# An attention opening with a choice per score job: distances added on TensorE or a mask multiplied on VectorE, under a new written order

## The chip, the core and the metric

The kernel runs on one core of one Trainium2 chip. A core has TensorE for matrix products (PE in the profile, with PEld for its loads of weights), VectorE (DVE), ScalarE (ACT), GpSimd (POOL) and SyncE (SP). Every engine works through its own queue in order and waits on semaphores for the others. Data come from the chip's memory by DMA; GpSimd issues the loads that change the number type on their way, SyncE and ScalarE the plain ones. The metric is the device time of the program in microseconds (us). Three runs of the kernel before took 213.77 to 213.87 us, with a median of 213.77; the profiled execution has a span of 212.0 us.

## The reference

There are two steps. The first is attention over 4 batches of 8 heads, 768 positions, head size 64, in which a query sees the 96 keys up to its own position and the first 8 keys of the sequence. A penalty grows with the distance:

```
rel  = pos[:, None] - pos[None, :]
keep = (pos[None, :] < n_global) | ((rel >= 0) & (rel < n_local))
dist = where(is_global & ~is_local, n_local, abs(rel))
scores = q @ k.T / sqrt(64) - slope[head] * dist,  -1e9 where not keep
a = exp(scores - max) / sum
attn = a @ v
```

The second is a feed-forward step on the result, seen as 3072 tokens of 512 values: `h = max(x @ w_in, 0)`, then `(h * h) @ w_out`, with a hidden width of 2048. All inputs and the output are float32; the kernel computes in float16 with float32 sums.

## The kernel before, in words

**Tiling.** The sequence of one batch is six tiles of 128 positions. A query tile needs two key tiles only: its own and "the one before", a mix (kb and vb) whose first 32 rows are the start of the sequence with its global keys and whose other 96 rows come from the preceding tile. Work goes by halves of a batch, three tiles each, eight halves in all. In every half attention is followed by the first layer (hps, L560), relu (hr, L584), square (h, L595) and second layer (yps, L609). From the second batch on, the attention of one half is spread between the matrix products of the previous half.

**The opening** is the first batch, both halves, with nothing to hide behind at first. It is cut into small jobs by tile, named by letter, tile and part, and the constant `OPENING` is the order in which TensorE gets them:
- `T` (turn_tile, L669): the q and k tiles are transposed on TensorE, and copied to qk by ScalarE and VectorE. T0 does tiles 0 and 1, which come in by plain loads and are cast on VectorE or ScalarE.
- `S..o` and `S..b` (score_tile): the scores of a tile against its own keys and against the tile before. ScalarE takes exp (L734). Distance and mask go in by one of two ways. Where `added` is true, eight matmuls (L714) of slope_id (a diagonal with the head's slope) and dmask16 (the distances, with a big number where masked) put the penalty into the sum ahead of the eight matmuls of q and k (L721); exp then writes the weights ph at once. Where it is false, exp writes ex, and two products on VectorE (L742) multiply it by the table mask. The eight matmuls of q and k use 64 rows of the array each, two at a time; all others use 128.
- `V` (fix_v, L202): copies that make vb for a tile.
- `A` (attend_tile, L760): weights times values, two head pairs at a time, then reciprocal (L770) and product (L772) on VectorE give tm.
- `X` (tile_to_x, L787): tm is transposed into xt.
- `F`, `G`, `D`, `E` (layer1, L560): first layer for some tiles and one quarter (F, D) or eighth (G, E) of the hidden width; quarter c needs the load c of w_in.

**Loads.** The constant `LOADING` is the order in which GpSimd issues the loads of q, k and v tiles (128 KB each as they land) and of the four quarters of w_in (c0 to c3). Four loads of w_out follow. Eight semaphores serve these loads in turn, so the ninth load waits until the first has landed. Two plain loads each from ScalarE and SyncE bring the first two tiles of q and k.

**The planner.** `Plan` decides everything else. Each operation has a cost in us for each engine that may do it, operations it needs, and a rank. `run` takes again and again the operation with the earliest possible start, ties by rank, on the engine where it ends first, and so fixes engine and order of all operations. TensorE's jobs and the loads stay in their written order. A first load that is a q or k tile has rank -3, the index tables (iota, L233 and L235) have rank -2, other loads a rank of their place among TensorE's jobs. From the iota come ident (L239), which the transposes need, then the distances (L244 to L255), slope_id, dmask16 and the masks (L271). The planner also puts fillers ahead of a job of TensorE (`warm`, L213 and L216): products of zeros that keep the array busy while it would idle, as many as its idle time by the plan allows up to 24 us, reckoned for the very first job from a fixed 1.0 us and halved in the first us. The fillers need ident and stand in the queue, so they run however late the job is by then.

Of the kernel before, what the change touches and what calls it, by code (L numbers as in the profile page):

```python
# [16 lines left out]

OPENING = """T0 T2 S0o S1o S2b V1 S1b A00 T3 V2 A01 S2o A10 S3o A11 A21 T4 X11 X01 S3b A20 X00 T5 X21 S4o  # L20
X20 X10 F1 S4b A31 G11 V3 G10 G01 F0 A41 X31 A30 G00 S5b A40 F3 X30 G30 F2 X41 V4 X40 S5o
G21 E10 E00 E11 A50 G20 A51 X50 G31 X51 E01 D0 D1"""

LOADING = """v1 q2 k2 k3 q3 v0 v2 q5 q4 k4 k5 c1 v3 c0 v4 c3 c2 v5"""

# [14 lines left out]
class Plan:  # L44
# [6 lines left out]


    HOP = 0.08

    def __init__(self, warm_from, warm_until):
        self.warm_from, self.warm_until = warm_from, warm_until
        self.queues = {"PE": [], "LOAD": []}
        self.rest = []
        self.free = {e: 0.75 for e in ("ACT", "DVE", "POOL", "SP")}
        self.landed = 4.2  # L60
        self.rank = 0
        self.banks = [[] for _ in range(8)]

    def pe(self, cost, emit, needs=(), takes=0, lag=0.24):
        self.rank += 1
        op = Op({"PE": cost}, emit, needs, self.rank, lag)
        op.takes, op.users = takes, [[op] for _ in range(takes)]
        self.queues["PE"].append(op)
        return op
# [11 lines left out]
        self.rest.append(op)  # L81
        return op

    def load(self, dur, emit, needs=(), rank=None, lag=2.6):
        rank = self.rank + 0.5 if rank is None else rank
        op = Op({"POOL": 0.92}, emit, needs, rank, lag, land=dur)
        self.queues["LOAD"].append(op)
        return op

    def ready(self, op):  # L90
        t = 0.0
        for n in op.needs:
            if n.done is None:
                return None
            t = max(t, n.done + self.HOP)
        if getattr(op, "takes", 0):
            banks = self.idle_banks(op.takes)
            if banks is None:
                return None
            t = max(t, banks[-1][0] + self.HOP)  # L100
        return t + op.wait

    def idle_banks(self, n):
# [5 lines left out]
    def run(self):  # L109
        order = []  # L110
        while self.rest or any(self.queues.values()):
            best = None
            for op in [q[0] for q in self.queues.values() if q] + self.rest:
                r = self.ready(op)
                if r is None:
                    continue
                e = min(op.costs, key=lambda e: max(r, self.free.get(e, 0.0)) + op.costs[e])
                c = (max(r, self.free.get(e, 0.0)), op.rank, e, op)
                if best is None or c[:2] < best[:2]:
                    best = c  # L120
            start, _, e, op = best
            end = start + op.costs[e]
            idle = self.free.get(e, self.warm_from)
            taken = self.idle_banks(op.takes) if getattr(op, "takes", 0) else []
            self.free[e] = end
            op.done = end + op.lag
            if op.land is not None:
                self.landed = max(end + 1.45, self.landed) + op.land
                op.done = self.landed + op.lag
            for q in self.queues.values():  # L130
                if q and q[0] is op:
                    q.pop(0)
                    break
            else:
                self.rest.remove(op)
            self.spare = 0.0
            for (_, i), users in zip(taken, op.users if taken else ()):
                self.banks[i] = users
            self.now = [i for _, i in taken]
            if taken and start < self.warm_until:  # L140
                self.spare = start - 0.1 - max(idle, taken[-1][0])
                self.spare *= 0.5 if start < self.warm_from + 5.0 else 1.0
            op.emit(e)
            order.append((start, end, e, op))
        return order
# [3 lines left out]
def kernel(  # L149
# [152 lines left out]
    def list_loads(x):  # L302
        r0 = x.half * HALF
        prev = halves[x.hb - 2] if x.hb >= 2 else None
        before = (prev.turned if prev else []) + ([*halves[x.hb - 1].turned, prev.x_ops[NPAIR - 1]] if x.hb > 3 else [])
        vbefore = [halves[x.hb - x.half - 3].attended[-1]] if x.hb >= 4 else []

        def rows(src, name, t, rank=None):
            def emit(e):
                dst = (x.bt.v[:, x.half * HT + t, :, 0:D] if name == "v"  # L310
                       else staged(x, name)[:, t, :, :])
                dma = nc.gpsimd.dma_start(out=dst, in_=src[x.b, :, r0 + t * P:r0 + (t + 1) * P, :]  # L312
                                          .rearrange("h p d -> p h d"))
                if x.hb > 3 and name == "sq" and t == 0:
                    for turn in halves[x.hb - 1].turns + halves[x.hb - 2].turns[-1:]:
                        behind(dma, turn)
                if name == "sk":
                    x.last_load = dma
            return plan.load(0.86, emit, vbefore if name == "v" else before, rank,
                             1.6 if x.hb == 0 else 2.6)  # L320

        if x.half == 0:
            def start(e):
                new_batch(x.bt)
                nc.vector.memset(x.bt.v[:, :, :, D:D + 1], 1.0)
            x.bt.op = plan.add({"DVE": 0.1}, start, vbefore, rank=0)
        if x.hb > 1:
            x.q_in = [rows(q, "sq", t) for t in range(HT)]
            x.k_in = [rows(k, "sk", t) for t in range(HT)]
            x.v_in = [rows(v, "v", t) for t in range(HT)]  # L330
        else:
            x.k_in, x.q_in, x.v_in = [None] * HT, [None] * HT, [None] * HT
            for t in range(HT):
                r = x.half * HT + t
                if r > 1:
                    for src, name, key, ops in ((k, "sk", "k", x.k_in), (q, "sq", "q", x.q_in)):
                        load_jobs[f"{key}{r}"] = lambda src=src, name=name, ops=ops, t=t: (
                            ops.__setitem__(t, rows(src, name, t, -3 if not plan.queues["LOAD"]
                                                    else None)))
                load_jobs[f"v{r}"] = lambda t=t: (  # L340
                    x.v_in.__setitem__(t, rows(v, "v", t)), x.v_in[t].needs.append(x.bt.op))
            return
        for l in x.v_in:
            l.needs.append(x.bt.op)
        x.bt.v_in = [*getattr(x.bt, "v_in", []), *x.v_in]
# [37 lines left out]
    def fix_v(bt, t0, t1):  # L383
        def emit(e):
            copy(e, bt.vb[:, t0 - 1:t1 - 1], bt.v[:, t0:t1])
            copy(e, bt.vb[0:GR, t0 - 1:t1 - 1], bt.v[0:GR, 0:1].to_broadcast(
                [GR, t1 - t0, H, D + 1]))
        op = plan.add({"DVE": 0.85}, emit, [bt.v_in[0], *bt.v_in[t0:t1]],
                      wait=0.0 if bt is batches[0] else 4.0)
        for t in range(t0, t1):  # L390
            bt.vb_ops[t] = op
# [56 lines left out]

    def score(x, k):
        for unit in [UNITS[x.half][u] for u in TOGETHER[x.half][k]]:  # L450
            score_unit(x, unit, unit[0] == UNITS[x.half][TOGETHER[x.half][k][0]][0])

    def score_unit(x, unit, fresh):
        bt, sp = x.bt, []

        def emit(e):
            sp.extend(bank([P, 4, P], FP32, "sp", h) for h in range(2))
            warm(sp[0].rearrange("p i c -> p (i c)"))
            for i, (a, r, before) in enumerate(unit):
                for h in range(2):  # L460
                    rows = slice(h * D, (h + 1) * D)
                    lhsT = (bt.kb[rows, a, r - 2, :] if before and r > 1
                            else bt.qk[rows, 1, r - before, a, :])
                    nc.tensor.matmul(sp[h][:, i, :], lhsT=lhsT, rhs=bt.qk[rows, 0, r, a, :],  # L464
                                     start=True, stop=True)
        job = plan.pe(0.182 * fresh + 0.057 * 4, emit,
                      [o for a in {a for a, _, _ in unit} for o in x.qk_ops[a]], 2)
        weigh_unit(x, unit, job, sp)

    def weigh_unit(x, unit, job, sp):  # L470
# [227 lines left out]
                copy(e, bt.kb[:, :, u - 1, 0:GR], bt.qk[:, 1, 0, :, 0:GR])  # L698
            kb_ops[u] = plan.add({"DVE": 0.65, "POOL": 1.2}, fix, [tile_ops[u][1], tile_ops[0][1]])

    def score_tile(r, before):
        bt = batches[0]
        st = tiles.setdefault(r, {"weighs": []})
        added = r < HT
        c0 = 2 * P if before else 0 if r == 0 else P

        def emit(e):
# [15 lines left out]
        needs = list(tile_ops[r]) + (slope_ops if added else [])  # L723
        if before:
            needs += [kb_ops[r - 1]] if r > 1 else tile_ops[r - 1]
        job = plan.pe(0.182 + NPAIR * 0.07 + added * H * 0.056, emit, needs, 2)
        exps = []
        st["ph", before] = phat_p.tile([P, 2, NPAIR, P], FP16, name="ph0", tag="ph0")
        for h in range(2):
# [18 lines left out]
    def attend_tile(r, a0):  # L748
# [13 lines left out]
        needs = st["weighs"][a0 // 2::2] + [bt.v_in[r]]  # L762
        if r > 0:
            needs.append(bt.vb_ops[r - 1] if r > 1 else bt.v_in[0])
        job = plan.pe(4 * len(kinds) * 0.035, emit, needs, 1)

        def norm(e):
            av = st["av", a0]
# [9 lines left out]
    def tile_to_x(r, a0):  # L778
        x, t, st = halves[r // HT], r % HT, tiles[r]

        def emit(e):
# [4 lines left out]
            for i in range(2):  # L786
                nc.tensor.transpose(out=trx[:, i, :], in_=st["tm", a0][:, i, :, :],  # L787
                                    identity=ident)
        job = plan.pe(2 * 0.07, emit, [st["norm", a0]], 1)
        op = plan.after(job, {"ACT": 0.29, "DVE": 0.25}, lambda e: copy(  # L790
            e, x.xt[:, a0:a0 + 2, t * P:(t + 1) * P], st["trx", a0]))
        for a in (a0, a0 + 1):
# [55 lines left out]
    for r in range(NT):  # L848
        jobs[f"T{r}"] = lambda r=r: turn_tile(r, 2 if r == 0 else 1)
        jobs[f"V{r}"] = lambda r=r: fix_v(batches[0], r, r + 1)  # L850
        jobs[f"S{r}o"] = lambda r=r: score_tile(r, False)
        jobs[f"S{r}b"] = lambda r=r: score_tile(r, True)
        for i in range(2):
            jobs[f"A{r}{i}"] = lambda r=r, i=i: attend_tile(r, 2 * i)
            jobs[f"X{r}{i}"] = lambda r=r, i=i: tile_to_x(r, 2 * i)
# [64 lines left out]
```

The softmax here doesn't subtract the row's maximum and nothing guards it: scores larger than these inputs give would overflow.

## Time and profile before

| | |
|---|---|
| median of three runs | 213.77 us |
| span of the profiled execution | 212.0 us |
| TensorE busy | 206.4 us, 97% |
| VectorE, ScalarE, GpSimd busy | 116.3, 122.5, 66.5 us |
| first transposes of T0 start | 5.89 us |
| first second-layer matmuls start | 44.11 us |

The page gives the time for which each engine was busy, then the chain of work that ended last. For a question about an opening of 44 us in a span of 212 the timeline of one engine is the better view: each line is a group of equal instructions with its start, its length, the line of the code, the operation, what is written and read, and in brackets the idle time before it and what ended that. A matmul's length includes the way through the array, and one starts before the last has ended; so the time that a group takes is read from the start of one group to the start of the next. 56 ns from start to start is a product of 128 columns at full rate.

### The profile page before, as it was taken

The page shows a single profiled execution, that of the slowest core. Times are in us where ns is not written, and L with a number is a line of the kernel's source. Part 1 is how long each engine was busy: PE and PEld are TensorE (multiplying, and loading weights), DVE is VectorE, ACT ScalarE, POOL GpSimd, SP SyncE. Part 2 cuts the span into 40 slices and gives each one's busy share as a digit, 9 for nine tenths or more (in the row PEclk, how much of TensorE's full clock was granted, in tenths as well). Part 3 has the DMA queues.
Part 4 walks back from the last instruction along what each step waited for, and adds up shares of the span by engine and source line. Part 5 has one row for each costly group of instructions (what it writes and reads, how often), then busy time and mean ns, then how long its engine had stood idle before and what let it go on. Part 6 is the DMA issues. An engine that isn't in the chain of part 4 may idle for free.

```text
span 212.0 us, 4795 instructions
## 1 busy us (share of the span) xinstructions
PE 206.4 (97%) x1902; PEld 127.6 (60%) x1902; DVE 116.3 (55%) x332; ACT 122.5 (58%) x252; POOL 66.5 (31%) x82
## 2 busy tenths in 40 slices
PE   6999999999999999999999999999999999999994
PEld 7877898755554665456644665456644665455553
DVE  8679878434681678319860778218860777114300
ACT  6899897735741994148811994248811994247421
POOL 8997343594001930094008600095000000000000
PEclk9999999999999999999999999999999999999999
DMA  6999999999954999599988995399941100320012
GB/s 175 167 164 197 199 198 209 163 154 169 179 162 136 118 152 145 136 121 178 142 112 128 168 152 111 91 125 174 153 120 77 53 19 19 90 99 2 0 53 99
DMA packets 106343, 27.06 MB, mean 128 GB/s; under 512 B 96976, under 2 KB 103376, under 8 KB 106320
## 3 DMA queue, kind: packets, MB, share of 16 engines
q0 software_dynamic: 74944, 13.11, 80.0%
q1 hardware_dynamic: 30320, 13.11, 27.4%
q10 hardware_dynamic: 1056, 0.52, 0.8%
q8 instruction: 15, 0.25, 0.5%
q14 instruction: 8, 0.07, 0.1%
HBM read 27.26 MB, written 6.29 MB: 158 GB/s over the span
## 4 chain that ended last, share of the span: by engine, by line
PE 88%; POOL 6%; DMA 5%; DVE 0%; ACT 0%; issue 0%; POOLq 0%
PE hps L560 39%; PE yps L609 38%; DMA w_in_sb<-in_moe_w_in_dram 5%; PE sp L464 4%; PE av L519 4%; POOL v L312 2%; POOL sk L312 2%; POOL sq L312 2%; PE yps L637 2%; PE trp L411 1%; PE av L760 1%; POOL w_in_sb L369 0%; PE trx L787 0%; PE sp L721 0%; DVE ident L239 0%; ACT y L200 0%
## 5 line engine op out<-in xcount | busy, mean ns | idle before, releaser
L560 PE MATMUL hps<-xt,w_in_sb 128*128 128x384 f16 (+2 forms) x608 | 88.0, 301 | 0.1
L609 PE MATMUL yps<-w_out_sb,h 128*128 128x512 f16 x368 | 83.0, 379 | 0.0
L560 PEld LDWEIGHTS <-w_in_sb 128*128 128x128 f16 x608 | 53.9, 98 | 26.9 <-DMA w_in_sb<-in_moe_w_in_dram 0.4
L584 ACT ACTIVATE hr<-hps 128x384 f16<-128x384 f32 (+1 forms) x107 | 55.3, 525 | 13.8 <-PE hps L560 12.0
L609 PEld LDWEIGHTS <-h 128*128 128x128 f16 x368 | 34.9, 98 | 39.0
L200 ACT COPY y<-yps 128x512 f32<-128x512 f32 (+1 forms) x25 | 14.2, 568 | 66.5 <-PE yps L609 56.8
L595 DVE TENSOR_TENSOR h<-hr 128x768 f16<-128x768 f16 (+1 forms) x70 | 35.4, 521 | 24.5 <-ACT hr L584 24.0
L312 POOL DMA_DIRECT2D sq<-in_q_dram x22 | 19.5, 897 | 67.1 <-DMA xt<-tm 63.9
L477 ACT ACTIVATE ex<-sp 128x512 f16<-128x512 f32 x66 | 35.1, 624 | 1.2 <-PE sp L464 1.2
L586 DVE TENSOR_SCALAR hr<-hps 128x384 f16<-128x384 f32 x15 | 8.3, 554 | 38.7 <-PE hps L560 38.7
L312 POOL DMA_DIRECT2D v<-in_v_dram x24 | 21.5, 927 | 4.7 <-DMA w_out_sb<-in_moe_w_out_dram 3.7
L497 DVE TENSOR_TENSOR phat<-ex,mask 128x1024 f16<-128x1024 f16 (+1 forms) x36 | 20.3, 598 | 2.1 <-ACT ex L477 2.1
L312 POOL DMA_DIRECT2D sk<-in_k_dram x22 | 19.5, 910 | 3.4 <-DMA w_out_sb<-in_moe_w_out_dram 2.9
L529 DVE TENSOR_TENSOR tm<-av,rec 128x384 f16<-128x384 f32 x24 | 13.4, 558 | 0.8
L202 DVE COPY vb<-v 128x520 f16<-128x520 f16 (+1 forms) x32 | 10.2, 318 | 3.2 <-DMA v<-in_v_dram 2.7
L519 PEld LDWEIGHTS <-phat 128*128 128x128 f16 x240 | 9.8, 98 | 3.1
L519 PE MATMUL av<-v,phat 128*128 128x65 f16 x144 | 10.9, 194 | 0.0
L519 PE MATMUL av<-vb,phat 128*128 128x65 f16 x96 | 10.1, 194 | 0.0
L464 PEld LDWEIGHTS <-qk 64*128 64x128 f16 x168 | 6.3, 94 | 4.6 <-issue 3.7
L464 PE MATMUL sp<-qk 64*128 64x128 f16 x168 | 8.8, 218 | 0.0
L202 DVE COPY kb<-qk 128x96 f16<-128x96 f16 (+4 forms) x56 | 7.9, 205 | 0.8 <-ACT qk L200 0.4
L527 DVE RECIPROCAL rec<-av 128x6 f32<-128x6 f32 x24 | 4.7, 195 | 6.7 <-PE av L519 6.2
(66 smaller groups left out, 137.8 us busy)
## 6 DMA issues: line engine op xcount, KB each, us to landing
out_dram<-y SPq DMA_DIRECT2D x23, 256.0 KB, 2.2
v<-in_v_dram POOLq DMA_DIRECT2D x24, 128.0 KB, 7.0
sq<-in_q_dram POOLq DMA_DIRECT2D x22, 128.0 KB, 5.7
sk<-in_k_dram POOLq DMA_DIRECT2D x22, 128.0 KB, 6.3
w_in_sb<-in_moe_w_in_dram POOLq DMA_DIRECT2D x4, 512.0 KB, 10.5
w_out_sb<-in_moe_w_out_dram POOLq DMA_DIRECT2D x4, 512.0 KB, 15.7
y<-in_k_dram ACTq DMA_DIRECT2D x2, 256.0 KB, 4.5
y<-in_q_dram SPq DMA_DIRECT2D x2, 256.0 KB, 4.0
```

What stands on the lines that cost most here:

```text
L200: nc.scalar.copy(out=out, in_=in_)
L202: eng(e).tensor_copy(out=out, in_=in_)
L312: dma = nc.gpsimd.dma_start(out=dst, in_=src[x.b, :, r0 + t * P:r0 + (t + 1) * P, :] .rearrange("h p d -> p h d"))
L464: nc.tensor.matmul(sp[h][:, i, :], lhsT=lhsT, rhs=bt.qk[rows, 0, r, a, :], start=True, stop=True)
L477: nc.scalar.activation(out=st["ex"][:, h], in_=sp[h], func=AF.Exp, scale=scale)
L497: eng(e).tensor_tensor(out=x.phat[a][:, :, t0:t0 + n], op=ALU.mult, in0=st["ex"][:, :, i0:i0 + 2 * n].rearrange("p e (t b) c -> p e t (b c ...
L519: nc.tensor.matmul(av[:, h, j, :], lhsT=lhsT, rhs=rhs, start=not before, stop=before or r == 0)
L529: nc.vector.tensor_tensor(out=st["tm"].rearrange("p t e d -> p e t d"), in0=av[:, :, :, 0:D], in1=rec[:, :, :, None].to_broadcast([P, 2, H ...
L560: nc.tensor.matmul(st["ps"][:, i * n:(i + 1) * n], lhsT=w_in_sb[:, kk, m * P:(m + 1) * P], rhs=x.xt[:, kk, c0:c1], start=kk == 0, stop=kk ...
L584: nc.scalar.activation(out=o, in_=i, func=AF.Relu)
L595: eng(e).tensor_tensor(out=x.h2[:, m0:m0 + width, c0:c1], in0=hr, in1=hr, op=ALU.mult)
L609: nc.tensor.matmul(st["ps"], lhsT=x.h2[:, m, j * P:(j + 1) * P], rhs=w_out_sb[:, m, :], start=m == 0, stop=m == NFT - 1)
```

## The change

`score_tile` gets `added` from the name of the job: a plus sign in `OPENING` (S0o+) means that TensorE adds the distances, none that VectorE multiplies by the mask. Before, the tile's number decided it. The order in `OPENING` and `LOADING` is written anew. The copies for vb in the first batch may go to GpSimd where the planner finds that this ends earlier. And the planner's costs are set anew: score jobs, attend jobs and transposes, a saving where two half-row jobs meet, the lag of a load until it can be used, and a load that waits for the eighth load before it.

It is meant to use whichever of TensorE and VectorE has room at each score job, and to give the planner a truer picture to order by.

```diff
-OPENING = """T0 T2 S0o S1o S2b V1 S1b A00 T3 V2 A01 S2o A10 S3o A11 A21 T4 X11 X01 S3b A20 X00 T5 X21 S4o
-X20 X10 F1 S4b A31 G11 V3 G10 G01 F0 A41 X31 A30 G00 S5b A40 F3 X30 G30 F2 X41 V4 X40 S5o
-G21 E10 E00 E11 A50 G20 A51 X50 G31 X51 E01 D0 D1"""
+OPENING = """T0 T2 S0o+ S2b T3 S1b+ S1o+ V2 A01 S2o+ S3o+ A10 A11 V1 S3b+ A21 A20 A00 T4 X21 X11 X01 X10
+T5 X20 S4o X00 A30 A31 S4b S5b F0 G00 S5o X30 X31 G01 G10 G11 F2 V3 A40 F1 A41 G21 V4 G20 F3
+X40 A50 A51 X41 G30 E10 X50 E11 X51 E01 D1 G31 D0 E00"""
-LOADING = """v1 q2 k2 k3 q3 v0 v2 q5 q4 k4 k5 c1 v3 c0 v4 c3 c2 v5"""
+LOADING = """q2 k2 k3 q3 v0 q5 v2 v1 k5 q4 k4 v3 c0 c1 c2 v4 c3 v5"""
...
     HOP = 0.08
+    SWITCH = 0.12
...
-    def load(self, dur, emit, needs=(), rank=None, lag=2.6):
+    def load(self, dur, emit, needs=(), rank=None):
         rank = self.rank + 0.5 if rank is None else rank
+        lag = 2.25 if len(self.queues["LOAD"]) < 5 else 2.85
...
+        if op.land is not None and len(self.loads) >= 8:
+            t = max(t, self.loads[-8].done)
...
+            if e == "PE":
+                end -= self.SWITCH * (op.begins and self.half_rows)
+                self.half_rows = op.ends
...
-        op = plan.add({"DVE": 0.85}, emit, [bt.v_in[0], *bt.v_in[t0:t1]],
+        op = plan.add({"DVE": 0.85, "POOL": 1.7} if bt is batches[0] else {"DVE": 0.85}, emit, [bt.v_in[0], *bt.v_in[t0:t1]],
...
-        job = plan.pe(0.182 * fresh + 0.057 * 4, emit,
-                      [o for a in {a for a, _, _ in unit} for o in x.qk_ops[a]], 2)
+        job = plan.pe(0.36, emit, [o for a in {a for a, _, _ in unit} for o in x.qk_ops[a]], 2,
+                      begins=True, ends=True)
...
-    def score_tile(r, before):
+    def score_tile(r, before, added):
...
-        added = r < HT
...
-        job = plan.pe(0.182 + NPAIR * 0.07 + added * H * 0.056, emit, needs, 2)
+        job = plan.pe(0.38 + added * 0.53, emit, needs, 2, begins=not added, ends=True)
...
-        job = plan.pe(4 * len(kinds) * 0.035, emit, needs, 1)
+        job = plan.pe(4 * len(kinds) * 0.0305, emit, needs, 1)
...
-        job = plan.pe(2 * 0.07, emit, [st["norm", a0]], 1)
+        job = plan.pe(2 * 0.06, emit, [st["norm", a0]], 1)
...
-        jobs[f"S{r}o"] = lambda r=r: score_tile(r, False)
-        jobs[f"S{r}b"] = lambda r=r: score_tile(r, True)
+        for added in ("", "+"):
+            jobs[f"S{r}o{added}"] = lambda r=r, added=added: score_tile(r, False, bool(added))
+            jobs[f"S{r}b{added}"] = lambda r=r, added=added: score_tile(r, True, bool(added))
```

More of the change, by code (lines that the diff above doesn't have):

```diff
@@ L60, in __init__, with pe @@
         self.landed = 4.2
+        self.loads = []
+        self.half_rows = False
         self.rank = 0
         self.banks = [[] for _ in range(8)]
-    def pe(self, cost, emit, needs=(), takes=0, lag=0.24):
+    def pe(self, cost, emit, needs=(), takes=0, lag=0.24, begins=False, ends=False):
         self.rank += 1
         op = Op({"PE": cost}, emit, needs, self.rank, lag)
+        op.begins, op.ends = begins, ends
         op.takes, op.users = takes, [[op] for _ in range(takes)]
@@ L129, in run @@
                 op.done = self.landed + op.lag
+                self.loads.append(op)
             for q in self.queues.values():
@@ L318, in emit @@
                     x.last_load = dma
-            return plan.load(0.86, emit, vbefore if name == "v" else before, rank,
-                             1.6 if x.hb == 0 else 2.6)
+            return plan.load(0.86, emit, vbefore if name == "v" else before, rank)
         if x.half == 0:
@@ L450, in score, with score_unit @@
         for unit in [UNITS[x.half][u] for u in TOGETHER[x.half][k]]:
-            score_unit(x, unit, unit[0] == UNITS[x.half][TOGETHER[x.half][k][0]][0])
-    def score_unit(x, unit, fresh):
+            score_unit(x, unit)
+    def score_unit(x, unit):
         bt, sp = x.bt, []
```

## The prediction

> **What bounds the kernel now.** I began with the busy times of the page, went to the chain that ended last, and then took the opening apart on the timeline of TensorE.
>
> ```profile
> PE 206.4 (97%) x1902; PEld 127.6 (60%) x1902; DVE 116.3 (55%) x332; ACT 122.5 (58%) x252; POOL 66.5 (31%) x82
> PE 88%; POOL 6%; DMA 5%; DVE 0%; ACT 0%; issue 0%; POOLq 0%
> ```
>
> TensorE is busy 97% of the span and is 88% of the chain. The rest of the chain, POOL and DMA, lies in the first 23 us. After 36.25 us I find no pause between matmul starts longer than the change of row grouping, so whatever the opening gains or loses passes to the end whole. The timeline of TensorE shows where the opening loses time (start, us, then the group; a start is when the group began):
>
> ```profile
> 5.89 0.63 PE L669 MATMUL trp<-ident,sq 128*128 128x128 f16 x4
> ...
> 7.60 0.89 PE L216 MATMUL trp<-ident,zero 128*128 128x128 f16 x13
> 8.32 0.39 PE L669 MATMUL trp<-ident,sq 128*128 128x128 f16 x4
> 9.11 0.40 PE L669 MATMUL trp<-ident,sk 128*128 128x128 f16 x4 [0.40 <-DMA sk<-in_k_dram]
> 9.35 0.61 PE L714 MATMUL sp<-dmask,slope_id 128*128 128x128 f16 x8
> 9.89 0.40 PE L721 MATMUL sp<-qk 64*128 64x128 f16 x8
> 10.22 0.62 PE L714 MATMUL sp<-dmask,slope_id 128*128 128x128 f16 x8
> ...
> 44.11 5.34 PE L609 MATMUL yps<-w_out_sb,h 128*128 128x512 f16 x24
> ```
>
> T0's 16 transposes take 5.89 to 7.60, 107 ns each; the 13 fillers after them take 0.72 us, 56 ns each. T2's second half then waits: 8.32 + 4 x 0.056 = 8.55, but it starts at 9.11, 0.56 us later. The list of waits for the first 60 us names what holds the weight loads:
>
> ```profile
> PEld L669 <- DMA sk<-in_k_dram: 0.8, 2, 0.6
> PEld L787 <- DVE tm L772: 0.5, 2, 0.3
> PEld L560 <- DMA w_in_sb<-in_moe_w_in_dram: 0.4, 1, 0.4
> ```
>
> Taken as pauses between matmul starts, from T0's end (7.60) to the first second-layer matmul (44.11) these are: sk 0.57 and 0.24, tm 0.21 twice, w_in 0.27, and 0.15 + 0.04 in attend jobs: 1.69 us idle. Fillers are 0.84. So of 36.51 us, 33.98 are work, and **at most 2.5 us can be won** if the work stays.
>
> The timelines of GpSimd and of the chain show the supply:
>
> ```profile
> 0.84 0.34 POOL L233 IOTA dist<- 128x256 f32 x1 [0.39 <-POOLq L901]
> 1.14 0.13 POOL L235 IOTA pidx<- 128x1 f32 x1
> 1.67 1.04 POOL L312 DMA_DIRECT2D v<-in_v_dram  x1 [0.40 <-DVE ident L239]
> 2.70 0.91 POOL L312 DMA_DIRECT2D sq<-in_q_dram  x1
> ```
>
> ```profile
> 13.07 9.78 DMA w_in_sb<-in_moe_w_in_dram
> 22.90 1.94 PE hps L560 x24
> ```
>
> The iota comes ahead of the first load, and the second w_in quarter lands at about 22.9.
>
> **What the Trainium skill says.** (1) "TensorE: Matmul & The Clock Gate", Part 1: the array runs at half rate until a free-running window of about 3.4 us has been busy. The trace agrees in kind: 107 ns a transpose until 7.6, 56 after, 5.9 us after the first filler at 1.67. (2) "DMA: Bandwidth & Descriptors", Queues, rings and completion order: each DMA engine takes turns between queues, packet by packet. The trace shows no even turns: the software queue's first load is issued by 2.71, yet from 2 to 5 us only the hardware queues moved data, and from 6 to 8 the software queue alone moved a steady 154 GB/s. (3) "GPSIMD Engine Reference", 4.1 Engine selection: one-input elementwise work is roughly line-rate on GpSimd. No copy on GpSimd is in this trace.
>
> **The change, part by part.**
>
> *Added distances.* Before, five score jobs add them (40 rows of L714): S0o, S1o, S1b, S2o, S2b. After, six: S0o, S1b, S1o, S2o, S3o, S3b. TensorE gets 8 x 0.056 = +0.45. VectorE loses one net job of two products (L742), 2 x 0.38 = -0.75 between 17 and 33 us. Changing the row grouping costs about 0.10 on entry (9.35 + 0.45 = 9.80, seen 9.89) and 0.12 on exit; S2b now follows S0o's half-row matmuls and S5b follows S4b, which saves 2 x 0.22 = 0.44. Net work: 0.0, so 34.0 us remain.
>
> *Order of loads.* v1 gives up the front. A tile takes 131 KB / 154 GB/s = 0.85 us. k2, third before, becomes second: landing 9.11 - 0.85 = 8.25, if the software queue is still held up by the hardware loads. The first w_in quarter moves behind one more value tile: about 19.3 (it was needed then, at 19.31) to at most 20.1-20.4. The second lands at 22.9 as now, the third 2.55 later at 25.4.
>
> *A side effect.* The first load has a rank of -3 when it is a q or k tile, so it is issued ahead of the iota (rank -2). The iota then waits 0.9 us for that issue on GpSimd's in-order queue, and ident, the fillers and the mask arithmetic wait with it: first filler 1.67 + 0.9 = 2.6. The planner's own arithmetic still asks for about 41 fillers before T0, since it reckons from a fixed 1.0 us: 41 x 0.107 = 4.3, T0 at 6.9 instead of 5.89. If the clock again rises at 7.6, six or seven transposes run at 107 ns and nine or ten at 56: T0 ends at about 8.13, **0.5 later**. The casts, done by about 6.5, hide.
>
> *T2 to S2b.* The planner's landing for k2 leaves about 9 fillers, 0.5 us. T2 at 8.63 finds k2 landed and ends at 9.08; S0o starts there, 0.27 ahead of 9.35. But S2b now comes second instead of third and needs kb of tile 1. In the trace T0's VectorE evacuations end 1.1 after T0, those of ScalarE 1.5, and the kb copies another 0.8: 7.60 + 1.5 + 0.8 = 9.93. Shifted by 0.53 this is 10.45 with T2's evacuation fitted in, while S0o is done at 9.08 + 0.76 = 9.84: **a new wait of 0.6**. Behind it T3 and every later job stand in TensorE's queue.
>
> *Middle.* From S2b to F0 I add 9.7 us of work (score jobs 0.22 to 0.89, attend jobs 0.14 or 0.25, transposes 0.45 or 0.11): F0 at 10.45 + 9.7 = 20.15, plus about 0.2 for k4, which comes eleventh instead of tenth. That meets the first w_in quarter at 20.1-20.4. Another 5.05 of work brings F2 to 25.4, on the landing of the third. From F2 18.1 of work remain: 25.5 + 18.1 = 43.6.
>
> *V on GpSimd.* On VectorE a pair of copies takes 0.7 to 0.86 us. The page puts one-input work at line rate and two-input work at about twice VectorE's time, so I bound it by 0.7 from below and 1.7 from above, and take 1.5 as an estimate. Queued behind it are loads, but eight are in flight by then and POOL already idles 1.6 to 1.9 us between them for w_in landings: that wait hides it. Nothing is charged.
>
> *New costs in the planner* (score units at 0.36, eight loads in flight, lags) move only the placing of operations. Nothing in the later stages waits now, so zero, with +0.3 as the other end.
>
> Sum: 44.11 becomes about 43.65 with 0.1 of small waits: **-0.45 us, 213.3**.
>
> **Rivals.**
> 1. *Fillers and cold clock eat it.* Should the clock rise late, at 9 instead of 7.6, T0 and T2 lose another 0.5 and S2b starts near 11.0. For it: T0's lateness is no longer covered by the wait for sk. Against: four equal runs. Time 213.8.
> 2. *A new wait in the middle: slower.* ScalarE is busy 4.64 of 5 us from 10 to 20 and VectorE 4.61 of 5 from 15 to 20; seven score jobs in a run need 14 exponentials of 0.49 and hold two banks each. One job's lag (1.0) on top of the forecast gives 43.65 + 1.0 = 44.65: 214.3. Against: VectorE has 0.75 less to do.
> 3. *The software queue starts earlier with its first issue*, by up to 0.83 us, so that all landings shift; S2b's wait shrinks when evacuations go well and the w_in floor drops: 1.2 won, 212.6. Against: the hardware loads hold it up at 5.2 to 5.9.
>
> **How the numbers follow.** Forecast 0.42, rival 1 0.22, rival 2 0.20, rival 3 0.16. The forecast lies just beyond 0.2% (0.43 us): 0.3 of its 0.42 and rival 3 are faster, 0.46. Same: 0.12 of the forecast and most of rival 1, 0.30. Slower: rival 2 and the tail of rival 1, 0.24. The range reaches from rival 3 to rival 2: 212.6 to 214.3. It takes in the copy (nil), the later stages (+0.3) and the clock (+0.5).
>
> **What would show it.** First load ahead of the iota; first filler near 2.6; T0 near 6.9; a pause of about 0.6 ahead of S2b's L721; F0 near 20.3 and F2 near 25.4, both released by w_in; first L609 matmul near 43.65. It is wrong if T0 starts at 5.9 as now, if the software queue moves data by 3 to 4 us, or if pauses over 0.3 released by ScalarE or VectorE stand between 12 and 20.

## The result and the profile after

The changed kernel takes 214.44 us (median of five runs; a sixth, in which TensorE was slow from beginning to end, took 548 us and is left out) against 213.77 before: a ratio of 1.0032, 95% interval 1.0018 to 1.0046. It is slower by 0.7 us; 213.3 was forecast, and 214.44 lies just outside the range of 212.6 to 214.3. The profile shown here is of a second series of the same code, with a span of 212.6 us (212.0 before).

> The changed kernel as it is, for a profile in which TensorE runs at its usual rate. Theory 1 (the opening starts late: the first load goes ahead of the iota, and 41 fillers hold T0): first filler near 3.0 us, T0 at 7.3 to 7.5 instead of 5.9, T0's end at 8.2 to 9.1, first second-layer matmul near 44.7. Theory 2 (a stall in the middle, ScalarE or VectorE): T0 costs little, and pauses of over 0.5 us in sum released by ScalarE or VectorE stand between 12 and 22 us. Ratio 1.002 to 1.005.

This second series gave 214.59 us, ratio 1.0035 [1.0021, 1.0049]. Its page, first the busy times, then the chain by engine:

```profile
PE 205.7 (97%) x1909; PEld 127.6 (60%) x1909; DVE 116.3 (55%) x329; ACT 121.4 (57%) x251; POOL 67.9 (32%) x84
PE 94%; ACT 3%; POOL 1%; issue 1%; DVE 0%; POOLq 0%; ACTq 0%
```

The busy times have hardly moved, and they could not tell the two kernels apart. In the chain, DMA has vanished and ScalarE, which had 0%, has 3%: that is the first hint. The timeline of TensorE, in the same columns as before:

```profile
3.04 4.52 PE L227 MATMUL trp<-ident,zero 128*128 128x128 f16 x41 [3.04 <-DVE ident L250]
7.36 0.42 PE L679 MATMUL trp<-ident,sq 128*128 128x128 f16 x4
8.29 0.67 PE L227 MATMUL trp<-ident,zero 128*128 128x128 f16 x9
8.79 0.39 PE L679 MATMUL trp<-ident,sq 128*128 128x128 f16 x4
9.01 0.39 PE L679 MATMUL trp<-ident,sk 128*128 128x128 f16 x4
9.23 0.61 PE L723 MATMUL sp<-dmask,slope_id 128*128 128x128 f16 x8
...
10.43 0.40 PE L730 MATMUL sp<-qk,kb 64*128 64x128 f16 x8
...
21.67 1.93 PE L570 MATMUL hps<-xt,w_in_sb 128*128 128x128 f16 x24
...
44.78 1.46 PE L619 MATMUL yps<-w_out_sb,h 128*128 128x512 f16 x6
```

The second-layer matmuls begin at 44.78 instead of 44.11, and this 0.67 is as large as the difference of the medians. The wait for the k tile (0.56 before) is gone: T2's second half follows its first after 0.22. From T0's end to the second layer it is 44.78 - 8.29 = 36.49 us; before it was 36.51. So the pauses that went came back elsewhere, and T0's end moved from 7.60 to 8.29. By this sum alone the late T0 would be the whole loss; the first experiment asks whether it is. The list of waits of the weight loads says where to look (us in total, times, longest):

```profile
PEld L769 <- ACT ph L743: 0.6, 2, 0.4
PEld L730 <- ACT qk L211: 0.4, 1, 0.4
```

TensorE now waits for exponentials and for the evacuation of transposes, both by ScalarE. And GpSimd, which issues the loads, begins thus:

```profile
1.24 1.02 POOL L323 DMA_DIRECT2D sq<-in_q_dram  x1 [0.80 <-POOLq L911]
```

The first load is ahead of the iota (which follows at 2.35), as forecast, but it begins at 1.24, where the iota had begun at 0.84.

### The profile page after: what moved, and what is told of

Same layout as the page of the kernel before. It is cut to its first block, busy times and chain, and to the rows that moved or that the text cites. A ratio compares the mean times of both kernels' runs of the same rounds, so it can differ in the third digit from the quotient of the medians.

```text
span 546.4 us, 4811 instructions
## 1 busy us (share of the span) xinstructions
PE 540.2 (99%) x1909; PEld 241.1 (44%) x1909; DVE 119.6 (22%) x329; ACT 127.3 (23%) x251; POOL 67.8 (12%) x84
## 4 chain that ended last, share of the span: by engine, by line
PE 99%; POOL 0%; issue 0%; ACT 0%; DVE 0%; POOLq 0%
PE hps L570 42%; PE yps L619 40%; PE sp L474 4%; PE av L529 4%; PE yps L647 2%; PE trp L227 1%; PE trp L679 1%; PE sp L723 1%; PE av L769 1%; PE sp L730 1%; PE trp L421 1%; PE trx L796 1%; POOL sq L323 0%; PE sp L224 0%; POOL dist L244 0%
## 5 line engine op out<-in xcount | busy, mean ns | idle before, releaser
L570 PE MATMUL hps<-xt,w_in_sb 128*128 128x384 f16 (+2 forms) x608 | 232.3, 613 | 0.0
L619 PE MATMUL yps<-w_out_sb,h 128*128 128x512 f16 x368 | 223.5, 836 | 0.0
L570 PEld LDWEIGHTS <-w_in_sb 128*128 128x128 f16 x608 | 99.5, 172 | 116.8 <-issue 102.9
L619 PEld LDWEIGHTS <-h 128*128 128x128 f16 x368 | 62.4, 173 | 139.4 <-issue 135.8
L596 DVE TENSOR_SCALAR hr<-hps 128x384 f16<-128x384 f32 (+1 forms) x16 | 9.0, 566 | 136.7 <-PE hps L570 136.7
L529 PEld LDWEIGHTS <-phat 128*128 128x128 f16 x240 | 21.9, 147 | 10.3 <-issue 9.2
L529 PE MATMUL av<-v,phat 128*128 128x65 f16 x144 | 22.5, 289 | 0.0
L474 PE MATMUL sp<-qk 64*128 64x128 f16 x168 | 19.0, 366 | 0.0
L474 PE MATMUL sp<-qk,kb 64*128 64x128 f16 x96 | 15.4, 371 | 0.0
L227 PE MATMUL trp<-ident,zero 128*128 128x128 f16 x50 | 7.6, 373 | 3.0 <-DVE ident L250 3.0
```

What stands on the lines that cost most here:

```text
L227: nc.tensor.transpose(out=ps[:, 0:n], in_=zero[:, 0:P], identity=ident)
L529: nc.tensor.matmul(av[:, h, j, :], lhsT=lhsT, rhs=rhs, start=not before, stop=before or r == 0)
L570: nc.tensor.matmul(st["ps"][:, i * n:(i + 1) * n], lhsT=w_in_sb[:, kk, m * P:(m + 1) * P], rhs=x.xt[:, kk, c0:c1], start=kk == 0, stop=kk ...
L619: nc.tensor.matmul(st["ps"], lhsT=x.h2[:, m, j * P:(j + 1) * P], rhs=w_out_sb[:, m, :], start=m == 0, stop=m == NFT - 1)
```

## The experiments

All ratios are to the kernel before, measured beside each kernel. Differences in us from the changed kernel are taken from its second series, 214.59; against the first, 214.44, they are 0.15 smaller. "F0" is the first first-layer matmul, "layer 2" the first second-layer one, both from the trace.

### Is it the late start?

My theory was first that the load ahead of the iota delays the fillers, T0 and all that follows. The rival was a wait in the middle.

```diff
-                            ops.__setitem__(t, rows(src, name, t, -3 if not plan.queues["LOAD"]
+                            ops.__setitem__(t, rows(src, name, t, -1 if not plan.queues["LOAD"]
```

> Alone the rank of the first load is changed from -3 to -1, so that the iota goes ahead of it; 40 fillers before T0 instead of 41. Theory 1: T0 at 5.9 again, S2b about 1 us earlier, 0.6 to 1.2 us faster than the changed kernel and 0 to 0.5 us faster than the kernel before: 213.2 to 213.8. Theory 2: no more than 0.2 us from the changed kernel, 214.2 to 214.5.

Measured: 214.70, ratio 1.0041 [1.0028, 1.0054]. The iota came first, S2b started at 10.00, 0.4 us earlier, and yet F0 was at 21.96 and the time not better (TensorE of e1):

```profile
10.00 0.40 PE L730 MATMUL sp<-qk,kb 64*128 64x128 f16 x8 [0.29 <-DVE kb L213]
...
21.96 1.94 PE L570 MATMUL hps<-xt,w_in_sb 128*128 128x128 f16 x24
```

So undoing the late start alone won nothing, and my first theory fell. What held the work is on ScalarE's timeline (e1, 10 to 17 us):

```profile
15.79 1.57 ACT L743 ACTIVATE ph<-sp 128x512 f16<-128x512 f32 x3 [1.96 <-PE av L769]
```

and in the changed kernel itself, 10 to 22 us:

```profile
12.73 2.10 ACT L743 ACTIVATE ph<-sp 128x512 f16<-128x512 f32 x4
15.76 3.04 ACT L743 ACTIVATE ph<-sp 128x512 f16<-128x512 f32 x6 [0.93 <-PE av L769]
18.64 1.13 ACT L211 COPY qk<-trp 128x512 f16<-128x512 f16 x2
```

In both, the exponentials of S2o begin at 15.8, after an idle time of ScalarE which was 0.93 in one and 1.96 in the other, as though a floor stood there. What released them is an attend matmul, "PE av L769". An exponential needs no result of an attend job; it writes ph, and the attend job reads ph. So this should be a wait for a buffer. There are four of them:

```python
phat_p = ctx.enter_context(tc.tile_pool(name="phat", bufs=4))
st["ph", before] = phat_p.tile([P, 2, NPAIR, P], FP16, name="ph0", tag="ph0")
```

S0o, S2b, S1b and S1o fill the four. In the new order A00 comes only after A20, so S0o's weights are kept all the while. S2o must have what A10 and A11 give back, and those run here (e1, TensorE, 13 to 16.5 us):

```profile
15.08 0.64 PE L769 MATMUL av<-v,ph 128*128 128x65 f16 x16 [0.57 <-DMA v<-in_v_dram]
```

A10 waits for the values of tile 1, v1. The new `LOADING` has v1 eighth; before it was first.

A second experiment on the start asked whether fewer fillers help. The time from which the planner reckons the fillers ahead of its first job was set from 1.0 to 2.6 us, which leaves 27 of them.

```diff
-plan = Plan(1.0, 24.0)
+plan = Plan(2.6, 24.0)
```

> The first load stays ahead of the iota; the planner reckons fillers from 2.6 us instead of 1.0, which leaves 27 before T0 instead of 41. Theory 1: T0 at 6.2 to 6.5 (by then its casts are done), 0.5 to 1.0 us faster than the changed kernel, near 213.6. If the late ident matters by the mask work behind it and not by the fillers, or theory 2 holds: within 0.2 us of the changed kernel.

Measured: 214.24, ratio 1.0024 [1.0014, 1.0033]. T0 began at 5.89 again, but its transposes had pauses for casts and ran at about 107 ns until 8.37; S0o began at 9.32 instead of 9.23. In the profiled execution nothing was won at the start, F0 moving from 21.67 to 21.59. But that execution took 214.41, and the profiled one of the changed kernel 214.42, while the nine runs of e2 lie between 214.11 and 214.91: these two traces cannot show where the medians differ.

The other half of the order, the new loads under the old jobs:

```diff
-LOADING = """v1 q2 k2 k3 q3 v0 v2 q5 q4 k4 k5 c1 v3 c0 v4 c3 c2 v5"""
+LOADING = """q2 k2 k3 q3 v0 q5 v2 v1 k5 q4 k4 v3 c0 c1 c2 v4 c3 v5"""
```

> The kernel before with the new LOADING alone (so q2 first, ahead of the iota, and k2 one place earlier); order of TensorE's jobs, costs and added set as before. Theory 1: T0 at 7.3 to 7.5 here too, but k2 lands 0.85 earlier, and 0.2 to 0.8 us slower than before since the old order asks for c1 and not c0 first: 214.0 to 214.9. Theory 2: 213.5 to 214.0, since the middle is the old one.

Measured: 217.48, ratio 1.0169 [1.0155, 1.0183]. The old order begins the first layer with F1, which needs c1, now the fourteenth load (TensorE of e3, 7 to 24 us):

```profile
20.95 2.75 PE L213 MATMUL hps<-zero 128*128 128x512 f16 x12
```

2.75 us of fillers stand where F1 should. The two orders belong together: undoing one alone measures mostly the mismatch. It says little about the change.

### Is it the buffers?

```diff
-                x.phat0 = phat_p.tile([P, 2, NPAIR, P], FP16, name="ph0", tag="ph0")
+                x.phat0 = phat_p.tile([P, 2, NPAIR, P], FP16, name="ph0", tag="ph0", bufs=7)
...
-        st["ph", before] = phat_p.tile([P, 2, NPAIR, P], FP16, name="ph0", tag="ph0")
+        st["ph", before] = phat_p.tile([P, 2, NPAIR, P], FP16, name="ph0", tag="ph0", bufs=7)
```

> The changed kernel with seven buffers for the weights ph of a score job instead of four; the order of every engine stays. Theory 3 (four ph buffers are full with S0o, S2b, S1b and S1o, since A00 comes late; S2o's exp waits until A10 and A11 have read theirs): ScalarE's idle 0.93 us before 15.76 goes, A20's and S4o's waits go, F0 starts at 20.5 to 20.9 instead of 21.7, 0.7 to 1.2 us faster than the changed kernel: 213.3 to 213.9. Theory R (ScalarE has too much to do as such): within 0.2 us of the changed kernel, 214.4 to 214.7.

Measured: 214.25, ratio 1.0020 [1.0013, 1.0027]. (The first of the two places is where the later batches use the same buffers.) On ScalarE the idle time ahead of S2o is gone (e4, 10 to 22 us):

```profile
12.55 5.04 ACT L743 ACTIVATE ph<-sp 128x512 f16<-128x512 f32 x10
```

Ten exponentials now run one after another. So the wait was for a buffer: shown. But only 0.34 us came of it. A10 still stood at 15.05, for v1, and a new idle time of 0.36 appeared behind the exponentials, for the transposes of T4, whose k tile k4 landed at about 17.5. Undoing two things at a time, the iota's place and the buffers (in both places, as in e4):

```diff
-                            ops.__setitem__(t, rows(src, name, t, -3 if not plan.queues["LOAD"]
+                            ops.__setitem__(t, rows(src, name, t, -1 if not plan.queues["LOAD"]
-        st["ph", before] = phat_p.tile([P, 2, NPAIR, P], FP16, name="ph0", tag="ph0")
+        st["ph", before] = phat_p.tile([P, 2, NPAIR, P], FP16, name="ph0", tag="ph0", bufs=7)
```

> Iota ahead of the first load and seven ph buffers. Theory 3: the 0.7 to 0.8 us that S0o gained by the iota alone is kept by ScalarE (S2o's exps at 13.8 instead of 15.8), but A10 stands in TensorE's queue until v1 lands at 15.0 and S3b behind it: F0 at 20.3 to 20.7, 213.2 to 213.6. Theory R: 214.4 or more, like the iota alone.

Measured: 214.28, ratio 1.0018 [1.0011, 1.0024]: no better. A10 waited 0.71 for v1, and F0 was at 21.39 as in e4.

### Is it the loads?

v1 alone, moved from eighth to sixth:

```diff
-LOADING = """q2 k2 k3 q3 v0 q5 v2 v1 k5 q4 k4 v3 c0 c1 c2 v4 c3 v5"""
+LOADING = """q2 k2 k3 q3 v0 v1 v2 q5 k5 q4 k4 v3 c0 c1 c2 v4 c3 v5"""
```

> The changed kernel with v1 sixth among the loads instead of eighth. Theory 3: A10 is then held by the exps of S1o, which end at 14.83, and starts no more than 0.1 earlier: within 0.3 us of the changed kernel. If v1's landing (14.94) alone set the middle: 0.5 us or more faster.

Measured: 214.50, ratio 1.0030 [1.0019, 1.0041]: within the intervals no change. Then v1 sixth together with the two edits of e6:

> All three: iota first, seven ph buffers, v1 sixth. Theory 3: A10 at about 14.1, F0 at 20.0 to 20.4, then held by the landing of the first w_in quarter or of k4: 212.9 to 213.4, faster than the kernel before by 0.4 to 0.9. If w_in or k4 land later than I think: F0 no earlier than 20.5, 213.4 to 213.7.

Measured: 214.24, ratio 1.0017 [1.0008, 1.0025]: no better either. The start is early, the buffers are free and v1 is there, and now everything arrives at the next gate early and waits (TensorE of e7, then its ScalarE and its VectorE):

```profile
17.49 0.40 PE L679 MATMUL trp<-ident,sk 128*128 128x128 f16 x4 [0.46 <-DMA sk<-in_k_dram]
```

```profile
17.92 1.07 ACT L211 COPY qk<-trp 128x512 f16<-128x512 f16 x2 [1.08 <-PE trp L679]
```

```profile
18.15 0.42 DVE L781 TENSOR_TENSOR tm<-av,rec 128x256 f16<-128x256 f32 x1 [1.31 <-PE trx L796]
```

All three engines wait for k4, the eleventh load: ScalarE 1.08 us, VectorE 1.31. Before, it was tenth, and T4's k half began at 16.42 after a wait of 0.24. T4, T5, S5b and F0 follow it in TensorE's queue; F0 comes 3.84 us after k4 (21.33 - 17.49). In the changed kernel T4's k half stands at 17.74, 0.25 behind this landing, and F0 3.93 after it: k4 was about to hold it too, and only the later wait hid that. So q4 and k4 go ahead of q5 and k5, with v1 sixth, seven buffers and the iota first kept:

```diff
-LOADING = """q2 k2 k3 q3 v0 q5 v2 v1 k5 q4 k4 v3 c0 c1 c2 v4 c3 v5"""
+LOADING = """q2 k2 k3 q3 v0 v1 v2 q4 k4 q5 k5 v3 c0 c1 c2 v4 c3 v5"""
```

> Iota first, seven ph buffers, v1 sixth, and now q4 and k4 eighth and ninth, ahead of q5 and k5. Theory 4 (with the buffers out of the way, the landing of k4 at 17.47, eleventh of the loads, holds T4, then T5, S5b and F0, 3.85 us behind it): k4 lands at about 15.8, T4's wait goes, F0 at 20.3 to 20.6, where the first w_in quarter lands: 213.0 to 213.5, at last faster than the kernel before. If the chain after T4 (T5's copies, S5b's kb) is set by VectorE or ScalarE and not by k4: no more than 0.3 us better than without it, 213.9 to 214.3.

Measured: **213.34, ratio 0.9980 [0.9973, 0.9986]**: faster than the kernel before. ScalarE of e8 (10 to 20 us) and TensorE:

```profile
11.61 5.23 ACT L743 ACTIVATE ph<-sp 128x512 f16<-128x512 f32 x10
16.92 1.07 ACT L211 COPY qk<-trp 128x512 f16<-128x512 f16 x2
```

```profile
16.28 0.39 PE L679 MATMUL trp<-ident,sq 128*128 128x128 f16 x4
16.50 0.39 PE L679 MATMUL trp<-ident,sk 128*128 128x128 f16 x4
...
20.57 1.61 PE L570 MATMUL hps<-xt,w_in_sb 128*128 128x128 f16 x21 [0.31 <-DMA w_in_sb<-in_moe_w_in_dram]
```

ScalarE goes on from exponentials to evacuations with no pause, T4's k half follows its q half at once, and F0, 1.1 us earlier than in the changed kernel, meets the first w_in quarter. That floor is about where the prediction had put it (20.1 to 20.4).

Which of the three repairs pay? These three runs combine the edits shown: the loads of e8 with seven buffers, alone, and with the iota first.

> The changed kernel (first load ahead of the iota) with seven ph buffers, v1 sixth, q4 and k4 eighth and ninth. Theory 4: T0 stays late, S0o at 9.2, so 0.3 to 0.8 us behind the same with the iota first: 213.4 to 214.0, about as the kernel before. If the late start is hidden wholly: equal to it within 0.2.

> The changed kernel with the loads alone mended (v1 sixth, q4 and k4 ahead of q5 and k5); four ph buffers, first load ahead of the iota. Theory 4: with four buffers S2o's exp still waits for A11, which now waits for S1o's exps only (14.83): T4 finds k4 landed as it did, so little is won: 214.2 to 214.5. If the order of loads is the whole cause: 213.3 to 213.6.

> Iota first and loads mended, four ph buffers. Theory 4: A10 follows S1o's exps at about 14.0, so ScalarE idles about 0.9 us there for want of a buffer, then all is 1 us earlier than with the iota alone: 213.5 to 213.9. If the buffers are needed as well: 214.0 or more. If they are not needed: 213.3 as with all.

| iota first | seven buffers | loads mended | median us | ratio to before |
|---|---|---|---|---|
| - | - | - | 214.59 | 1.0035 [1.0021, 1.0049] |
| yes | - | - | 214.70 | 1.0041 [1.0028, 1.0054] |
| - | yes | - | 214.25 | 1.0020 [1.0013, 1.0027] |
| - | - | yes | 214.60 | 1.0034 [1.0022, 1.0047] |
| yes | yes | - | 214.28 | 1.0018 [1.0011, 1.0024] |
| yes | - | yes | 214.10 | 1.0017 [1.0011, 1.0024] |
| - | yes | yes | 213.54 | 0.9994 [0.9986, 1.0003] |
| yes | yes | yes | 213.34 | 0.9980 [0.9973, 0.9986] |

Buffers alone give 0.34 us, loads alone nothing, both 1.05. The median of the loads alone is soft, since its eight runs fall into two groups, 214.09 to 214.39 and 214.82 to 214.99. The traces say the same when the start is left out: from S2b to F0 it is 11.24 us in the changed kernel, 11.08 with the buffers, 11.07 with the loads and 10.34 with both (TensorE of e15):

```profile
11.18 0.40 PE L730 MATMUL sp<-qk,kb 64*128 64x128 f16 x8
...
21.52 1.93 PE L570 MATMUL hps<-xt,w_in_sb 128*128 128x128 f16 x24
```

(This execution of e15 was the longest of its 13, with S2b 0.75 later than in the changed kernel, which gives the loads more time; in e8, with S2b early, it is 10.72, of which 0.31 is the wait for w_in.) They are two gates in a row, and whoever opens one only moves the wait to the other. With the loads mended and four buffers the wait is on ScalarE as before, 0.76 us in e16; with the iota first as well it is longer (ScalarE of e20):

```profile
15.01 2.06 ACT L743 ACTIVATE ph<-sp 128x512 f16<-128x512 f32 x4 [1.34 <-PE av L769]
```

The earlier start that the iota's place brings gives nothing while v1 is eighth (+0.1 and 0.0), and 0.5 and 0.2 with the loads mended, differences at the edge of the intervals. It looks as though, as long as v1's landing sets A10, an earlier start only lengthens the waits. One more move was tried against the last floor, the w_in quarter c0 a place earlier:

```diff
-LOADING = """q2 k2 k3 q3 v0 v1 v2 q4 k4 q5 k5 v3 c0 c1 c2 v4 c3 v5"""
+LOADING = """q2 k2 k3 q3 v0 v1 v2 q4 k4 q5 k5 c0 v3 c1 c2 v4 c3 v5"""
```

> All mended, and the first w_in quarter one place earlier, ahead of v3. F0 waited 0.3 us for it, so F0 at 20.3 to 20.4 instead of 20.57 and 213.0 to 213.2. If v3, now later, holds A40 or its copy delays GpSimd's loads: 213.4 or more.

Measured: 214.20, ratio 1.0021 [1.0012, 1.0030]: worse by 0.86 than without it. v3 gave up its place, and A30, which needs it, stands ahead of F0, now at 21.53 (TensorE of e21, 15 to 27 us):

```profile
20.40 0.19 PE L769 MATMUL av<-v,ph 128*128 128x65 f16 x1 [0.99 <-DMA v<-in_v_dram]
```

### The other parts of the change

The planner's costs and the copies on GpSimd alone, with orders, loads and added set as before (the first lines; the rest of the two constants is as before too):

```diff
-OPENING = """T0 T2 S0o+ S2b T3 S1b+ S1o+ V2 A01 S2o+ S3o+ A10 A11 V1 S3b+ A21 A20 A00 T4 X21 X11 X01 X10
+OPENING = """T0 T2 S0o+ S1o+ S2b+ V1 S1b+ A00 T3 V2 A01 S2o+ A10 S3o A11 A21 T4 X11 X01 S3b A20 X00 T5 X21 S4o
...
-LOADING = """q2 k2 k3 q3 v0 q5 v2 v1 k5 q4 k4 v3 c0 c1 c2 v4 c3 v5"""
+LOADING = """v1 q2 k2 k3 q3 v0 v2 q5 q4 k4 k5 c1 v3 c0 v4 c3 c2 v5"""
```

> The changed code with the order, the loads and the added set of the kernel before, so only the planner's new costs and the choice of GpSimd for V: 25 fillers before T2 instead of 13 by the new lag of loads. If the new costs are harmless: 213.6 to 214.0. If they misplace copies or fillers: 0.4 us or more slower than before.

Measured: 213.96, ratio 1.0008 [1.0002, 1.0015]: +0.2 us. If the parts add, the rest of the loss, about 0.5, is that of the new orders with the new added set. The new added set in the old order, here as it differs from e12:

```diff
-OPENING = """T0 T2 S0o+ S1o+ S2b+ V1 S1b+ A00 T3 V2 A01 S2o+ A10 S3o A11 A21 T4 X11 X01 S3b A20 X00 T5 X21 S4o
+OPENING = """T0 T2 S0o+ S1o+ S2b V1 S1b+ A00 T3 V2 A01 S2o+ A10 S3o+ A11 A21 T4 X11 X01 S3b+ A20 X00 T5 X21 S4o
```

> As the costs alone, with the added set of the changed kernel (S3o and S3b by TensorE, S2b by the mask) in the old order. TensorE has 0.45 more and 0.22 less for one change of rows, VectorE 0.75 less, and four ph buffers must hold one more job: 0 to 0.5 us slower than the costs alone. If the choice by itself pays through VectorE: 0.2 to 0.4 faster.

Measured: 216.06, ratio 1.0106 [1.0091, 1.0122]. This did not test what it was made for. The planner put the copies of V3 on VectorE ahead of other work, perhaps because it saw VectorE free sooner (VectorE, then TensorE of e13):

```profile
20.38 0.61 DVE L213 COPY vb<-v 128x520 f16<-128x520 f16 x2 [1.45 <-DMA v<-in_v_dram]
```

```profile
21.60 0.40 PE L796 MATMUL trx<-ident,tm 128*128 128x128 f16 x4 [0.80 <-DVE tm L781]
```

The copies wait 1.45 us for v3 at the head of an in-order queue, and the product that TensorE needs for the next transposes waits behind them. So the question was put again, in the mended order of e8:

```diff
-OPENING = """T0 T2 S0o+ S2b T3 S1b+ S1o+ V2 A01 S2o+ S3o+ A10 A11 V1 S3b+ A21 A20 A00 T4 X21 X11 X01 X10
+OPENING = """T0 T2 S0o+ S2b+ T3 S1b+ S1o+ V2 A01 S2o+ S3o A10 A11 V1 S3b A21 A20 A00 T4 X21 X11 X01 X10
```

> All mended (iota, seven buffers, loads), but with the added set of the kernel before: S2b added, S3o and S3b by the mask. TensorE 0.45 less for one job and 0.22 more for a change of rows, VectorE 0.75 more. If the choice of ways pays: 0.2 to 0.6 us slower than all mended (213.6 to 213.9). If TensorE is the scarcer: 213.0 to 213.3. F0 is held by w_in there, so equal is likely too.

Measured: 214.14, ratio 1.0017 [1.0010, 1.0023]: 0.80 slower than e8, and F0 at 21.31 instead of 20.57. TensorE spends 0.83 us there on fillers ahead of the X jobs behind T4, where e8 spends 0.11, and its weight loads still wait 0.6 for VectorE's products. In that order the new choice of jobs that TensorE adds, with what the planner makes of it, is worth 0.8 us. The copies for vb back on VectorE alone, again in e8:

```diff
-        op = plan.add({"DVE": 0.85, "POOL": 1.7} if bt is batches[0] else {"DVE": 0.85}, emit, [bt.v_in[0], *bt.v_in[t0:t1]],
+        op = plan.add({"DVE": 0.85}, emit, [bt.v_in[0], *bt.v_in[t0:t1]],
```

> All mended, but the copies for vb on VectorE alone. On GpSimd one pair took 1.3 us (21.4 to 22.7) beside loads that were waiting for others. My charge was nil, so equal within 0.2 us: 213.1 to 213.5. If GpSimd relieves VectorE where it counts: 0.3 or more slower.

Measured: 213.65, ratio 0.9995 [0.9988, 1.0002]: by the medians GpSimd's help is worth 0.3 there. Both profiled executions took 213.46, with layer 2 at 43.83 and 43.85, while the 21 runs of e18 reach from 213.35 to 214.18 and those of e8 only from 213.05 to 213.52. The 0.3 comes from the longer runs of e18, of which there is no trace. Last, seven buffers in the kernel before:

> The kernel before with seven ph buffers, as a control. There A00 and A01 come early and free S0o's buffer, and no exp waits for one: within 0.2 us of the kernel before. If the buffers help there too, 0.3 or more faster, and then they are a gain of their own and no mending of the change.

Measured: 213.74, ratio 1.0000 [0.9991, 1.0008]. The old order did not need them: the gain of e8 over the kernel before is not the buffers' own.

## Why the prediction was wrong

**The step that failed** is *Middle*: "From S2b to F0 I add 9.7 us of work ... F0 at 10.45 + 9.7 = 20.15, plus about 0.2 for k4". S2b came at 10.43, as forecast, and F0 at 21.67: 11.24 us later and not 9.9. From F0 to layer 2 it then took the 23.1 us of the forecast, so this 1.3 is, within 0.2, the whole distance from the forecast 43.65 to the measured 44.78. The sum counted what TensorE has to do, and not what each job must have before it can be done. Three things were missing. Four ph buffers were enough for the old order and not for the new one, which asks for a fifth before any has come free: ScalarE idles 0.93. v1, eighth in the new list, lands at about 15.0 and holds A10, which gives buffers back. And k4 lands at about 17.5, just ahead of T4, which it holds as soon as the buffers are there. With the buffers and the loads mended, F0 came 10.34 us after S2b (e15), so about 0.9 of the surplus of 1.3 is these; the remaining 0.4 is made of smaller pauses (T5 is 0.21 late between its halves in e8), for which I had allowed 0.1 in all. The pauses can be counted in the changed kernel's TensorE timeline:

```profile
15.05 0.65 PE L769 MATMUL av<-v,ph 128*128 128x65 f16 x16
...
16.90 0.20 PE L769 MATMUL av<-v,ph 128*128 128x65 f16 x1 [0.25 <-ACT ph L743]
...
19.83 0.40 PE L730 MATMUL sp<-qk 64*128 64x128 f16 x8 [0.25 <-ACT qk L211]
```

From start to start, A10 is 0.18 late, A20 0.42 late in its middle, T5 0.3, S4o 0.32: 1.2 of the 1.3 in all, so the work itself was summed about right. None is large, and the last starts from ScalarE's evacuations, which begin at 18.64 because its exponentials had been held until 15.76. Following a pause back to the engine that was itself waiting is what led to the buffer.

**Rival 2** had the right time, 214.3, and the right symptom, pauses released by ScalarE between 12 and 20. Its reason was wrong: it had ScalarE overloaded. ScalarE was idle for want of a buffer; with seven, the same ten exponentials ran through in 5.04 us. The prediction called the forecast wrong if such pauses over 0.3 showed, and they did. Rival 1, the late rise to full rate, did not set the changed kernel's profile (S2b at 10.43), but it came in e15's, with the rise at 9.0 and S2b at 11.18. Rival 3 did not come: in both kernels the software queue moved its first 0.06 MB between 5 and 6 us.

**What held.** 41 fillers, then 9. The k tile's wait gone. S0o 9.23 (9.08 forecast), S2b 10.43 (10.45). This last hit is partly luck: T0 began 0.5 later than forecast but ran almost wholly at full rate, and the wait ahead of S2b was shorter; in e4, e16 and e5, which have the same start, S2b came at 10.30, 10.56 and 11.07. The whole difference made in the opening and passed to the end. The copies on GpSimd: 1.31 us for a pair (GpSimd's timeline, the changed kernel; 1.67 in e8), inside the bounds of 0.7 to 1.7, with no wait of TensorE behind them:

```profile
21.33 1.31 POOL L213 COPY vb<-v 128x520 f16<-128x520 f16 x2
```

Here "GPSIMD Engine Reference", 4.1 Engine selection of the Trainium skill, which puts one-input work roughly at line rate, was too kind: VectorE took 0.61 to 0.75 for a pair in the same execution, and the measurement decides.

**Mis-sized.** T0 began at 7.36 and not at 6.9: the first load began at 1.24, and I had let it take the iota's place at 0.84. T0's end was 8.29 (8.13 forecast). "A new wait of 0.6" ahead of S2b became a filler of 0.22 and a shorter pause, since S0o had ended later. And this late start cost nothing by itself: e1 took it away, and the time stayed. It was hidden by the landing of v1; with buffers and loads mended it costs 0.2 (e15 against e8). Two slips in the working are small: 41 x 0.107 is 4.39 and not 4.3 (the fillers took 4.32), and 7.60 + 1.5 + 0.8 is 9.90 and not 9.93. *New costs in the planner* were charged nil with +0.3 as the other end; e12 measured +0.2, the copies included.

**What stays open.** Why e2's median is 0.35 lower; where GpSimd's 0.3 lies; and whether A00 moved up to A01, which would free a buffer without a larger pool, does as well as seven buffers. That order was not tried.

## What to carry to other kernels

A new order of jobs has to be checked against two lists besides the work: how many buffers of each kind are alive at each job, and where in the load order the last tile that it needs stands. In a trace, an engine "released" by a reader of its own output, from which it needs nothing, points to a wait for a buffer, however short the list of waits makes it look; more buffers are the test. When undoing one part shows nothing, look at what the work now runs into: here two gates in a row were worth 0.3 and 0.0 singly, and 1.05 together, and behind them stood a change that pays, by 0.2%.

## What the hardware showed that I had not expected

The moment at which TensorE goes to full rate moves between executions. By the spacing of the matmuls, 107 ns before and 56 after, it is 7.6 us in the kernel before, 7.4 in the changed one, 7.2 in e8, 8.4 in e2, 9.0 in e15 and 6.1 in e3. Over all 19 traces it lies between 4.3 (e22) and 9.0, that is 2.6 to 5.9 us after the first filler. The Trainium skill, "TensorE: Matmul & The Clock Gate", Part 1, speaks of a free-running window of about 3.4 us that must have been busy, so that the rise depends on where the window stands; the traces agree with that in kind, though the 2.6 of e22 lies below a full window. e15 and the changed kernel, alike in their first 10 us by the program (T0 at 7.36 in both), differ by 0.75 in S2b (11.18 and 10.43), of which 0.72 is there at the end of T0 (9.01 and 8.29), whose transposes ran at 107 ns in the one and almost all at 56 in the other. The profiled execution of e15 was also its longest, 214.28 against a median of 213.54. A single trace of an opening can therefore mislead by as much as the effect sought, and the medians decided wherever the two disagreed.
